# Attention and feed-forward kernel: dummy matmuls at the start, shared PSUM banks, q copies on ScalarE, fewer weight loads

## The chip, the cores and the metric

The kernel runs on one core of a Trainium2 chip. The metric is device time in microseconds (us), the median of several executions. The profile is of one execution; its span runs from the first to the last instruction and is shorter than the device time, by 1.7 to 3.8 us in the executions on record. "Clock" is the share of its full clock that TensorE was granted. Kernels are compared by a ratio: the mean time of one kernel's fast runs over that of the kernel before in the same rounds on the same chip, so it is not quite the ratio of the medians quoted beside it. 95% intervals are given in brackets.

## The reference

```python
# q, k, v: 4 batches x 8 heads x 768 positions x 64; heads 0, 2, 6 "retrieval", the others "streaming"
scores = q @ k.T / 8
mask   = causal                                        # retrieval heads
mask   = causal & (key < 4 | query - key < 64)         # streaming heads
a      = softmax(where(mask, scores, -1e9)) ; attn = a @ v
x      = attn, heads side by side: 3072 tokens x 512
h      = x @ w_in                                      # 512 -> 2048
out    = (max(h, 0) + alpha * min(h, 0)) @ w_out       # 2048 -> 512, fp32
```

## The kernel before

The work is cut into segments of one batch and two heads. Batch 0 is split into halves: segments 0 to 3 (kind "a") and 4 to 7 (kind "b"). Segments 8 to 19 are whole ("all"): 768 queries each. A segment passes through the engines like this: GpSimd casts q, k, v to bf16; TensorE transposes q and k; copies bring them from PSUM (the memory that TensorE writes to, in banks) to qT and kT; TensorE makes scores; ScalarE takes the exponential; VectorE multiplies the causal or window mask in; TensorE multiplies with v (`pav`); VectorE normalises (`xn`); TensorE transposes that, and VectorE copies it to xT. Blocks of the feed-forward are put between these pieces to fill TensorE.

The parts that the change and the argument touch:

```python
    def T_bank(nat, n, tag):                       # transposes of q or k
        tr = ps.tile([128, 1024], bf16, tag=tag, name="tr")
        for i in range(n):
            nc.tensor.transpose(tr[:, 128 * i:128 * (i + 1)], nat[:, i, :], ident)
        return tr

    def Tq(n):
        ...
        tr = T_bank(natq.pop(n), T, "mm0" if sg.kind == "a" else "tr")
        dst = qT[sg.seq % NK][:, sg.q0:sg.q1]
        if sg.kind == "all":
            nc.vector.tensor_copy(dst, tr[:, 0:S])
        else:
            nc.scalar.copy(...)

    def S_retr(n, hh, m):                          # scores of a retrieval head
        ...
        on_pe = sg.kind == "a"                     # mask added in PSUM by TensorE
        ...
        nc.scalar.activation(e[:, lo:hi], sc[:, 0:hi - lo], AF.Exp, scale=scale)
        for j in [] if on_pe else done:            # or multiplied by VectorE
            ej = e[:, sg.ro[j]:sg.ro[j] + RM[j]]
            nc.vector.tensor_tensor(ej, ej, mr[:, max(j - 1, 0), 0:RM[j]], op=ALU.mult)

    def AV(n, hh):
        pav = ps.tile([128, NT, D + 1], fp32, tag=f"pav{hh}", name="pav")
        ...
    def P2(t, s, quarter):                         # second product, and its output
        ...
            ot = work.tile([128, 512], fp32, tag="ot", name="ot", bufs=3)
            nc.scalar.copy(ot, po.pop(t))
            nc.sync.dma_start(out[r:r + 128, :], ot)
    ...                                            # main loop: casts for segment n + 2
            if i == 0:
                if 8 <= n + 2 < NSEG:
                    pre = [lambda n=n: cast(n + 2)]
```

The on_pe way matters later: TensorE adds a large negative number to the masked scores by one more matmul, so VectorE has no mask to multiply.

The softmax here doesn't subtract the row's maximum and nothing guards it: scores larger than these inputs give would overflow.

## Time and profile before

| | kernel before |
|---|---|
| device time, first three runs | 266.31 us (266.02 to 266.82) |
| span of the profiled execution | 263.8 us |
| TensorE busy | 238.1 us (90%) |
| VectorE, ScalarE, GpSimd busy | 181.3, 142.2, 68.1 us |
| TensorE idle in 5 to 22 us, 22 to 36, 36 to 60, 60 to 100 | 2.4, 2.3, 3.5, 5.9 us |

The lines behind these numbers are in the prediction. Read them in this order: the busy shares say that TensorE is the engine to free; the busy time by stretch says that its holes end at 100 us; its waits say who ends them.

### The profile page before, as it was taken

The numbers are of one execution on the slowest core, as the hardware profiler recorded it, in microseconds if no ns is written. First come the engines' busy times: TensorE is split into PE (matmuls) and PEld (weight loads), VectorE is DVE, ScalarE is ACT, GpSimd is POOL, SyncE is SP. The second block draws the span as 40 slices with busy tenths as digits, with TensorE's granted clock in tenths as the row PEclk, the third lists the DMA queues.
The fourth block names the chain that finished last, engine by engine and source line by source line (L and its number), as shares of the span: only waits on it lengthen the run. The fifth ranks groups of instructions, "written<-read, shape, count | busy, mean of one in ns | idle before, by whom it ended". The sixth has DMA issues, their size and how long they took to land.

```text
span 263.8 us, 5619 instructions
## 1 busy us (share of the span) xinstructions
PE 238.1 (90%) x2112; PEld 148.3 (56%) x2139; DVE 181.3 (69%) x483; ACT 142.2 (54%) x305; POOL 68.1 (26%) x122
## 2 busy tenths in 40 slices
PE   1897898978888879999999999999998999999994
PEld 1684345544766655655557855655557754456651
DVE  7897787557799776999528964997428946863310
ACT  2782675533675436686355646685446626644320
POOL 8799226524423422503113130500000000000000
PEclk9999999999999999999999999999999999999999
DMA  7989999999999978340121001000211011001212
GB/s 223 323 139 193 198 208 259 224 271 211 256 221 256 214 186 218 88 96 0 42 80 43 0 30 52 2 1 0 82 40 43 0 42 40 0 2 40 81 40 80
DMA packets 75275, 29.84 MB, mean 113 GB/s; under 512 B 63969, under 2 KB 72177, under 8 KB 75249
## 3 DMA queue, kind: packets, MB, share of 16 engines
q1 hardware_dynamic: 70448, 24.77, 37.2%
q0 software_dynamic: 4224, 4.19, 9.8%
q10 hardware_dynamic: 576, 0.53, 0.6%
q8 instruction: 16, 0.26, 0.5%
q14 instruction: 11, 0.08, 0.1%
HBM read 27.39 MB, written 6.29 MB: 128 GB/s over the span
## 4 chain that ended last, share of the span: by engine, by line
PE 63%; DVE 16%; DMA 7%; POOL 6%; ACT 4%; issue 3%; SPq 0%; POOLq 0%; ACTq 0%; DVEq 0%
PE mm L442 21%; PE mm L425 20%; PE sc L442 8%; DVE g L432 5%; PE pav L390 4%; DMA vf<-in_v_dram 4%; DMA kf<-in_k_dram 3%; PE sc L327 3%; PE tr L245 3%; DVE xn L397 2%; PE sc L359 2%; PE tr L405 2%; DVE eS L371 2%; ACT eR L334 2%; DVE eR L337 1%
## 5 line engine op out<-in xcount | busy, mean ns | idle before, releaser
L425 PE MATMUL mm<-xT,w_in_b 128*128 128x256 bf16 (+1 forms) x503 | 98.3, 325 | 3.8 <-DVE g L432 2.4
L432 DVE SCALAR_TENSOR_TENSOR g<-neg,oma,mm 128x512 bf16<-128x512 f32 (+1 forms) x128 | 77.3, 611 | 25.2 <-ACT neg L431 21.6
L431 ACT ACTIVATE neg<-mm 128x512 f32<-128x512 f32 (+1 forms) x128 | 62.6, 492 | 44.1 <-PE mm L425 40.8
L442 PE MATMUL mm<-w_out_b,g 128*128 128x512 bf16 x273 | 71.0, 379 | 0.8
L425 PEld LDWEIGHTS <-w_in_b 128*128 128x128 bf16 x512 | 47.6, 98 | 33.7 <-issue 5.0
L442 PEld LDWEIGHTS <-g 128*128 128x128 bf16 x384 | 34.8, 98 | 26.6
L334 ACT ACTIVATE eR<-sc 128x455 bf16<-128x455 f32 (+5 forms) x72 | 38.7, 552 | 18.8 <-PE sc L327 17.5
L366 ACT ACTIVATE eS<-sc 128x384 bf16<-128x384 f32 x60 | 28.8, 490 | 26.3 <-PE sc L359 24.1
L148 POOL CAST qb<-qf 128x768 bf16<-128x768 f32 (+1 forms) x16 | 12.5, 782 | 71.9 <-PE tr L245 65.0
L327 PE MATMUL sc<-qT,kT 128*128 128x268 bf16 (+16 forms) x141 | 25.8, 268 | 1.6 <-DVE kT L281 1.6
L337 DVE TENSOR_TENSOR eR<-eR,mr 128x128 bf16<-128x128 bf16 (+4 forms) x60 | 14.3, 257 | 16.6 <-ACT eR L334 16.5
L371 DVE TENSOR_TENSOR eS<-eS,ms 128x384 bf16<-128x384 bf16 x50 | 18.4, 375 | 8.5 <-ACT eS L366 8.1
L442 PE MATMUL sc<-w_out_b,g 128*128 128x512 bf16 x93 | 22.8, 379 | 0.1
L397 DVE TENSOR_TENSOR xn<-pav,rcp 128x448 bf16<-128x448 f32 (+2 forms) x40 | 21.8, 544 | 1.4
L359 PE MATMUL sc<-qT,kT 128*128 128x192 bf16 (+4 forms) x150 | 21.1, 234 | 0.4 <-ACT eS L366 0.4
L327 PEld LDWEIGHTS <-kT 128*128 128x128 bf16 x141 | 12.1, 99 | 11.8 <-DVE kT L281 2.0
L446 ACT COPY ot<-mm 128x512 f32<-128x512 f32 x18 | 10.6, 586 | 15.1 <-PE mm L442 14.7
L359 PEld LDWEIGHTS <-kT 128*128 128x128 bf16 x150 | 13.8, 99 | 6.0 <-issue 0.7
L149 POOL CAST kb<-kf 128x768 bf16<-128x768 f32 (+1 forms) x16 | 12.6, 786 | 11.2 <-PE tr L245 7.5
L390 PEld LDWEIGHTS <-eS 128*128 128x128 bf16 x270 | 11.6, 98 | 5.1 <-DVE eS L371 0.9
L407 DVE COPY xT<-tr 128x768 bf16<-128x768 bf16 (+2 forms) x20 | 9.5, 476 | 7.2 <-PE tr L405 7.0
L390 PE MATMUL pav<-vb,eS 128*128 128x65 bf16 x270 | 13.5, 194 | 0.7 <-DVE eS L371 0.4
(79 smaller groups left out, 199.3 us busy)
## 6 DMA issues: line engine op xcount, KB each, us to landing
out_dram<-ot SPq DMA_DIRECT2D x24, 256.0 KB
qf<-in_q_dram SPq DMA_DIRECT2D x12, 384.0 KB
kf<-in_k_dram SPq DMA_DIRECT2D x12, 384.0 KB
vf<-in_v_dram SPq DMA_DIRECT2D x24, 192.0 KB
w_in_b<-in_moe_w_in_dram POOLq DMA_DIRECT2D x4, 512.0 KB, 5.8
w_out_b<-in_moe_w_out_dram POOLq DMA_DIRECT2D x4, 512.0 KB, 13.1
qf<-in_q_dram SPq DMA_DIRECT2D x4, 256.0 KB
vf<-in_v_dram SPq DMA_DIRECT2D x5, 160.0 KB
```

The costliest lines, as they stand in the source:

```text
L327: nc.tensor.matmul(sc[:, a - lo:z - lo], kt[:, 128 * j:128 * (j + 1)], qt[:, c:c + z - a], start=True, stop=not masked)
L334: nc.scalar.activation(e[:, lo:hi], sc[:, 0:hi - lo], AF.Exp, scale=scale)
L337: nc.vector.tensor_tensor(ej, ej, mr[:, max(j - 1, 0), 0:RM[j]], op=ALU.mult)
L359: nc.tensor.matmul(sc[:, o:o + z - a], kt[:, 128 * j:128 * (j + 1)], qt[:, 124 * j + a:124 * j + z], start=True, stop=not on_pe)
L366: nc.scalar.activation(two, sc[:, 0:384].rearrange("p (s c) -> p s c", c=192), AF.Exp, scale=scale)
L371: nc.vector.tensor_tensor(two, two, ms5 if first == 4 else ms, op=ALU.mult)
L390: nc.tensor.matmul(pav[:, i, :], e[:, o:o + 128], vv[:, j, hh, :], start=(m == 0), stop=(m == len(terms) - 1))
L397: nc.vector.tensor_tensor(xn[n][:, lo:hi, 64 * hh:64 * hh + 64], pav[:, lo:hi, 0:D], rcp[:, lo:hi].to_broadcast([128, hi - lo, D]), op=ALU ...
L425: nc.tensor.matmul(psg[:, 0:w], w_in_b[:, a, 128 * f:128 * (f + 1)], xT[:, c, o:o + w], start=(c == 0), stop=(c == 3))
L431: nc.scalar.activation(neg[:, 0:w], psg[:, 0:w], AF.Relu, scale=-1.0)
L432: nc.vector.scalar_tensor_tensor(g_buf[t % 2][:, f, 0:w], neg[:, 0:w], oma[:, f:f + 1], psg[:, 0:w], op0=ALU.mult, op1=ALU.add)
L442: nc.tensor.matmul(po[t], g_buf[t % 2][:, f, 128 * s:128 * (s + 1)], w_out_b[:, f, :], start=(f == 0), stop=(f == 15))
```

## The change

Five things: 36 dummy matmuls during the first loads (so that the array's clock is up when the work begins), three PSUM banks in rotation for transposes and attention output together (instead of one bank for transposes and two for output), the q copies of whole segments on ScalarE, a reordered start of the first projection, and the weights in seven loads instead of eight, in another order.

```diff
-    def load_w_in(n):
+    def load_w_in(lo, hi):
...
+    def misc_tag():
+        n_misc[0] += 1
+        return f"m{n_misc[0] % 3}"
...
-        tr = ps.tile([128, 1024], bf16, tag=tag, name="tr")
+        tr = ps.tile([128, 1024], bf16, tag=tag or misc_tag(), name="tr")
...
-        tr = T_bank(natq.pop(n), T, "mm0" if sg.kind == "a" else "tr")
+        tr = T_bank(natq.pop(n), T, "mm0" if sg.kind == "a" else None)
...                                                 # Tk likewise
-            nc.vector.tensor_copy(dst, tr[:, 0:S])
+            nc.scalar.copy(dst, tr[:, 0:S])
...
-        pav = ps.tile([128, NT, D + 1], fp32, tag=f"pav{hh}", name="pav")
+        pav = ps.tile([128, NT, D + 1], fp32, tag=misc_tag(), name="pav")
...
+    warm = ps.tile([128, 512], fp32, tag="mm2", name="warm")
+    for i in range(36):
+        nc.tensor.matmul(warm[:, 0:128], ident, ident, start=True, stop=True)
     Tq(0)
...                                                 # w_in in three loads, then w_out, then the memsets
+    AV(3, 1)
+    for f in range(3):
+        P1(0, f, range(3))
+    X(3)
+    for f in range(3):
+        P1(0, f, range(3, 4))
+    for f in range(3, 6):
+        P1(0, f)
     nc.vector.tensor_copy(ms[:, 1, :], ms[:, 0, :])
...                                                 # three more mask copies
-    P1(0, 0, range(3))
-    P1(0, 1, range(3))
-    AV(3, 1)
-    P1(0, 2, range(3))
-    X(3)
-    ...
-    for f in range(3, 13):
+    for f in range(6, 13):
         P1(0, f)
```

More of the change, by code (lines that the diff above doesn't have):

```diff
@@ L231 @@
     oma = wpool.tile([128, 16], fp32, name="oma")
-    def load_w_in(n):
-        nc.gpsimd.dma_start(w_in_b[:, :, 512 * n:512 * (n + 1)],
-                            moe_w_in[:, 512 * n:512 * (n + 1)].rearrange("(a p) f -> p a f", p=128))
+    def load_w_in(lo, hi):
+        nc.gpsimd.dma_start(w_in_b[:, :, lo:hi], moe_w_in[:, lo:hi].rearrange("(a p) f -> p a f", p=128))
     def load_w_out(n):
@@ L239, in load_w_out @@
                             moe_w_out[512 * n:512 * (n + 1), :].rearrange("(a p) f -> p a f", p=128))
+    n_misc = [0]
+    def misc_tag():
+        n_misc[0] += 1
+        return f"m{n_misc[0] % 3}"
     def T_bank(nat, n, tag):
-        tr = ps.tile([128, 1024], bf16, tag=tag, name="tr")
+        tr = ps.tile([128, 1024], bf16, tag=tag or misc_tag(), name="tr")
         for i in range(n):
@@ L261, in Tk @@
         T = (sg.q1 - sg.q0) // 128
-        tr = T_bank(natk.pop(n), T, "mm1" if sg.kind == "a" else "tr")
+        tr = T_bank(natk.pop(n), T, "mm1" if sg.kind == "a" else None)
         for hh, h in enumerate(sg.heads):
@@ L402, in X @@
         nat = xn.pop(n)
-        tr = ps.tile([128, 1024], bf16, tag="tr", name="tr")
+        tr = ps.tile([128, 1024], bf16, tag=misc_tag(), name="tr")
         for i in sg.tiles:
@@ L483 @@
     cast_v(0)
+    load_w_in(0, 512)
     clear_e(nc.gpsimd, eS[1])
@@ L486 @@
     cast_v(1)
-    load_w_in(0)
+    load_w_in(512, 1024)
     cast_qk(3)
     cast_v(2)
-    load_w_in(1)
+    load_w_in(1024, 2048)
     clear_e(nc.gpsimd, eS[2])
     cast_v(3)
-    load_w_in(2)
-    load_w_in(3)
-    clear_k(nc.gpsimd, 4)
+    for i in range(4):
+        load_w_out(i)
     for i in range(NF):
         nc.gpsimd.memset(vf[i][:, 6, :, :], 0.0)
-    for i in range(4):
-        load_w_out(i)
+    clear_k(nc.gpsimd, 4)
     for n in range(4, 8):
@@ L516 @@
         if n == 0:
-            tra = ps.tile([128, 16], fp32, tag="tr", name="tra")
+            tra = ps.tile([128, 16], fp32, tag=misc_tag(), name="tra")
             nc.tensor.transpose(tra, alpha_r, ident_f)
             nc.vector.tensor_scalar(oma, tra, -1.0, 1.0, op0=ALU.mult, op1=ALU.add)
+    AV(3, 1)
[6 more added lines that the diff above has]
+        P1(0, f)
     nc.vector.tensor_copy(ms[:, 1, :], ms[:, 0, :])
@@ L526 @@
     nc.vector.memset(ms5[0:NSINK, 1, 148:152], 0.0)
-    P1(0, 0, range(3))
-    P1(0, 1, range(3))
-    AV(3, 1)
-    P1(0, 2, range(3))
-    X(3)
-    for f in range(3):
-        P1(0, f, range(3, 4))
-    for f in range(3, 13):
+    for f in range(6, 13):
         P1(0, f)
```

## The prediction

> **What bounds the kernel now.** I read the page's busy shares, then busy time by stretch, then TensorE's waits, then the timeline of TensorE, VectorE and ScalarE around each wait.
>
> ```profile
> PE 238.1 (90%) x2112; PEld 148.3 (56%) x2139; DVE 181.3 (69%) x483; ACT 142.2 (54%) x305; POOL 68.1 (26%) x122
> ```
>
> The span is 263.8 us (the device time of 266.31 adds a constant 2.5). TensorE is the bound: it executes one fixed order of matmuls, so the end moves by what its stalls and its slow clock lose, and by nothing else. Where are they?
>
> ```profile
> 5.00:22.00 17.00, 14.65 (x206) 12.26 (x208) 15.28 (x58) 12.55 (x29) 15.03 (x32) 1.00 1.06 231
> 22.00:36.00 14.00, 11.73 (x68) 5.39 (x67) 10.80 (x21) 7.12 (x14) 6.92 (x20) 1.00 1.21 205
> 36.00:60.00 24.00, 20.46 (x192) 12.03 (x194) 15.47 (x52) 12.86 (x29) 9.54 (x18) 1.00 1.14 243
> 60.00:100.00 40.00, 34.13 (x406) 24.92 (x411) 32.44 (x97) 21.53 (x53) 15.69 (x21) 1.00 0.96 225
> 100.00:199.00 99.00, 97.92 (x844) 59.27 (x856) 69.48 (x176) 58.10 (x119) 16.96 (x23) 1.00 0.17 49
> ```
>
> Columns: length, then busy time of PE, weight load, DVE, ACT, POOL. From 100 us on TensorE is full (97.92 of 99): nothing to win there. It has holes up to 100 us, and TensorE's own waits name them:
>
> ```profile
> PE tr L245 <- POOL qb L148: 5.4, 1, 5.4
> PE tr L245 <- DVE qT L254: 2.8, 4, 0.9
> PE tr L245 <- DVE xT L407: 2.6, 5, 0.9
> PE mm L425 <- DVE g L432: 2.4, 3, 1.1
> PE tr L405 <- DVE xn L397: 2.2, 4, 0.6
> ...
> PE tr L245 <- POOL vb L165: 0.8, 1, 0.8
> ```
>
> The first is the wait for the first load and cast. The next two are the single bank "tr": a transpose of q or k can't begin until the copy of the transpose before it has left the bank. The row "POOL vb" is one of these too: in the timeline the k transpose begins at 41.53, and the ScalarE copy that empties its bank ends at 41.12 + 0.37 = 41.49.
>
> ```profile
> 41.12 0.37 ACT L256 COPY qT<-tr 128x256 bf16<-128x256 bf16 x1
> ```
>
> The waits lose more than their idle time, since a transpose's modelled end overlaps the next start. Counting from issue to issue (start of the waiting instruction, less the start of the group before it and its count times the usual spacing), the stalls at "tr" are, in us: 1.00 (at 41.53), 0.67 (47.48), 1.01 (54.74), 0.63 (55.48), 0.66 (60.67), 0.85 (69.86), 1.14 (79.59), 0.84 (89.45), 0.81 (96.36), 0.81 (97.50), 0.36 (150.21). Sum 8.8.
>
> **The slow start.** Four transposes of q early, and the same four later; then VectorE while the early ones run:
>
> ```profile
> 8.81 0.63 PE L245 MATMUL tr<-ident,qb 128*128 128x128 bf16 x4
> 13.18 0.39 PE L245 MATMUL tr<-ident,qb 128*128 128x128 bf16 x4
> 7.23 0.62 DVE L281 COPY kT<-tr 64x512 bf16<-64x512 bf16 x1
> 10.73 0.65 DVE L506 MEMSET qT<- 128x144 uint32 x4
> 11.41 0.68 DVE L281 COPY kT<-tr 64x512 bf16<-64x512 bf16 x1
> ```
>
> The k transposes that follow begin at 9.24 and 13.40, so four take 0.43 early and 0.22 later: TensorE runs at half speed until about 11.7 us, although the granted-clock column says 1.00. But the second copy into kT begins at 11.41, though its transposes were over by 9.9: VectorE works through memsets without a hole from 5.4 on, and in the timeline it has none before 21.0.
>
> **What the Trainium skill says.** "TensorE: Matmul & The Clock Gate", Part 1, says that the array runs at half clock until some 3.4 us of sustained activity, and falls back after an idle window of about that length. The trace agrees: half speed, then full speed after roughly 4 us of unbroken work (7.9 to 11.7); the holes of about 1 us later don't bring it back. "ScalarE: Activation LUTs", What ACT_TABLE_LOAD costs, gives 186 ns + 0.833 ns per element for an ACTIVATE without pointer operands: 0.61 for 512 elements; the trace's qT copies took 0.59 (512) and 0.37 (256), so I extend those to about 0.81 for 768. "DMA: Bandwidth & Descriptors", Issuing engines are not separate DMA queues, says that all queues share 16 engines and interleave. The trace agrees in so far as the DMA share stays at 0.96 to 1.21 from 5 to 100 us with weights and q/k/v together. No page is needed for the bank wait: the trace has it.
>
> **The change, part by part.**
> Dummy matmuls: 36 of 128 columns at 0.108 each (0.43/4) are 3.9 us, begun when the identity is ready (1.4), over by 5.3; the first real transpose waits for a cast until 5.39 anyway. So they cost nothing, and TensorE then runs the next 6 us at twice the speed. What is it worth? In 7.9 to 11.7 about 1.9 us of TensorE time, but VectorE sets the pace of this stage: its order up to 22 us is unchanged in the built program, and it is full. TensorE gets early to the second segment's scores, which need the kT copy ending at 12.09 and began at 12.42. I give it 0.2 us.
>
> Order after the first batch: attention output of head pair 3 goes ahead of six partial projections, and four VectorE mask copies (22.84 to 24.22, that is 1.4 us) go behind the sixth g. Before, these copies held the reciprocal back to 24.22 and the output transposes to 24.99. Now nine partial projections (9 x 0.2155 = 1.9 us) come first; with the wait for the last exponential (22.5) I get transposes at 24.7: gain 0.3. But the copies now stand in the loop where a unit takes 0.862 on TensorE and g 0.75 on VectorE, with three banks in rotation, so hardly any slack (0.13). They take 0.8 to 1.4 there: loss 0.7. Net -0.4, a loss.
>
> Three shared banks: in the new rotation a bank comes back after three uses, so a transpose never waits for the one just before it, and the attention output gets banks whose readers are at least two steps back. All 8.8 us of stall lose their cause. What of it arrives? From 41 to 61 us VectorE is only two thirds busy, so of 3.97 I count 3.7. From 69 to 98 VectorE has no hole for 9 us at a time (67.7 to 77.1, 77.4 to 86.8): there TensorE, released earlier, meets VectorE at the next xn or mask, and the gain is what VectorE itself loses in work or idleness: 0.6, 0.75, 0.75 and 1.3 of 4.45, together 3.4. At 150: 0.2. Sum 7.3.
>
> q copies on ScalarE: 12 x 0.55 = 6.6 us off VectorE, 12 x 0.81 = 9.7 us onto ScalarE, which is 54% busy. It is what makes the 3.4 above possible (0.55 of each segment), so it is not counted again. After 100 us neither engine binds for long: 0.
>
> Weights in fewer parts: one issue less (0.74 on GpSimd), the first one 3 us earlier, w_out ahead of the memsets. GpSimd's work before the memset on which the later v loads wait changes by -0.74 - 1.65 + 2.98 = +0.6 us, and w_out is then ahead of those loads. But TensorE waits for no weight now, and the last casts of the second half end at 43.6 for transposes at 54.7. Value 0.
>
> Sum: 0.2 - 0.4 + 7.3 = 7.1 off. I keep about 15% back for waits that I don't see (ScalarE's longer copy ahead of an exponential, VectorE's order), so 6.1: 266.3 - 6.1 = **260.2 us**.
>
> **Rivals.** (a) VectorE becomes the bound of 60 to 100: it has 32.4 us of work in 40, less five q copies (2.8) 29.7; if its stretches without holes don't shrink, of 3.4 only half comes, and with the mask copies at their full 1.4 us the sum is 4: about 262.3. For it speaks the chain of waits, which has many VectorE pieces there; against it that TensorE's waits in it are for the two copies by name. (b) The warm clock counts in full: if VectorE's memsets are not what the first stage waits for, up to 1.9 us more: about 258.3. Against it stands the copy at 11.41. (c) Weights ahead of q/k/v make the second half's transposes wait at 36 to 55; each late load costs its lateness, 1 to 3 us: 261 to 263. Against it, 5 us and more of slack at each cast but the first.
>
> **Range and chances.** The stalls removed are certain as causes; what is open is how much is given back. 258.0 if the warm clock counts or nothing is given back, 263.0 if (a) and (c) both bite. 2% is 261.0, close above my figure: faster by over 2% 0.60, within 2% 0.39, slower 0.01.
>
> **What would show it right or wrong.** Right: TensorE's waits no longer name a q or k transpose waiting for qT or xT; early transposes 0.22 for four, yet the output of the first stage (TensorE's first projection, 22.0) moves by under 0.5; a stall of about 0.7 on "mm" behind g after the sixth unit; the stretch 36 to 100 shorter by about 7; a qT copy on ScalarE of about 0.81; the stretch from the last transposes to the end unchanged. Wrong: the first projection comes 1.5 us or more earlier (then VectorE wasn't the bound), TensorE's waits move to xn, kT or the exponentials with the same total, or casts wait for loads and transposes for casts.

## The result and the profile after

The changed kernel took 264.02 us (263.96 to 264.40, 4 runs) against 266.56 us for the kernel before in the same rounds: ratio 0.9908 [0.9885, 0.9931], that is 0.9% faster and within 2%. The span of the profiled execution was 262.4 us against 263.8: 1.4 us, where the medians differ by 2.5. (The profiled execution of the kernel before took 266.97 us, 3.2 more than its span; that of the changed kernel 264.40, 2.0 more. So about 1 us of the measured gain is not in these two profiles.) The prediction was 260.2 with a range from 258.0 to 263.0, so it is wrong by 3.8 us, and outside its range.

First, busy time by stretch of the changed kernel, with the columns of the prediction (length; PE, weight load, DVE, ACT, POOL; granted clock, DMA share, GB/s):

```profile
5.00:22.00 17.00, 14.58 (x212) 12.12 (x210) 15.29 (x58) 12.49 (x29) 15.03 (x33) 0.90 1.17 252
22.00:36.00 14.00, 12.01 (x69) 5.61 (x68) 9.94 (x21) 7.24 (x14) 6.17 (x17) 1.00 1.19 204
36.00:60.00 24.00, 22.82 (x225) 13.81 (x226) 16.81 (x57) 14.10 (x32) 11.50 (x21) 1.00 0.99 220
60.00:100.00 40.00, 32.60 (x380) 23.57 (x382) 32.79 (x92) 24.32 (x56) 13.66 (x19) 1.00 1.00 234
```

From 36 to 60 us TensorE is busy for 22.82 us where it was 20.46: that gain has come. From 60 to 100 us it is busy for 32.60, less than the 34.13 before, and VectorE, although 2.8 us of q copies have left it there, is no less busy (32.79 against 32.44).

TensorE's waits in the changed kernel (total, times, longest):

```profile
PE pav L395 <- DVE eS L376: 3.3, 5, 1.0
PE mm L430 <- DVE g L437: 2.6, 4, 1.1
PE sc L332 <- DVE kT L286: 1.9, 2, 1.6
PE tr L410 <- DVE xn L402: 1.6, 3, 0.5
PE warm L484 <- POOL ident masks.py:199: 1.4, 1, 1.4
PE pav L395 <- DVE eR L342: 1.3, 3, 0.5
PE sc L332 <- ACT eR L339: 1.1, 1, 1.1
```

No transpose of q or k waits for qT or xT any more. In their place stand waits for masked exponentials (eS, eR), that is, for VectorE and for what feeds it.

A third view makes the place of the loss plain: the start of the same matmuls in the timelines of several kernels, and by how many us each is earlier than in the kernel before. (X is the transpose of a segment's attention output, Tq the transpose of its q. The experiments are explained below.)

| start of | before, us | changed | six output buffers (e5) | casts moved too (e9) | masks on TensorE, q on VectorE (e15) | masks on TensorE in the kernel before (e17) | banks and masks alone (e18) |
|---|---|---|---|---|---|---|---|
| X of segment 3 | 24.99 | 0.37 | 0.37 | 0.35 | 0.38 | -0.05 | -0.05 |
| Tq of segment 4 | 36.44 | 0.13 | 0.13 | -0.02 | 0.13 | -0.04 | -0.04 |
| Tq of segment 8 | 60.67 | 3.61 | 3.78 | 3.40 | 3.61 | 0.27 | 3.37 |
| X of segment 8 | 66.26 | 3.61 | 3.77 | 3.16 | 3.55 | 0.22 | 3.31 |
| X of segment 9 | 75.92 | 1.15 | 2.54 | 2.31 | 3.91 | 0.34 | 3.67 |
| X of segment 10 | 85.66 | 0.31 | 1.48 | 1.98 | 4.28 | 0.86 | 4.04 |
| X of segment 11 | 95.16 | -0.21 | -0.17 | 1.97 | 4.77 | 1.35 | 4.52 |
| X of segment 12 | 102.88 | 0.97 | 1.01 | 3.15 | 5.94 | 1.34 | 5.70 |

In the changed kernel 3.6 us have been gained by 66 us, and 2.6 of them are lost by 103. From there to the end the two kernels run alike, but for another 0.4 us at the transposes near 150 us: the last X comes 1.38 us earlier, which is the difference of the spans. So the question is what took back the gain between 66 and 96 us.

The traces offered four suspects. **The output buffers**: an output copy on ScalarE stands for 1.48 us just there. It needs the buffer of the third output before it, whose transfer was issued late (at 60.93), behind loads that wait in the same queue. An exponential stands behind the copy. **The masks**: VectorE's masks became longer, at moments when GpSimd casts. **VectorE's queue as a whole**: from 67.5 to 75.2 us it has no hole. **The q copies**: on ScalarE one takes 0.80 us and stands ahead of the last exponential of a segment. A fifth one showed only in the experiments: **the clock** of the array.

Lines for the first two. ScalarE's output copy and TensorE's wait that follows from it, changed kernel, timeline (start, us, engine, line):

```profile
63.88 0.59 ACT L451 COPY ot<-mm 128x512 f32<-128x512 f32 x1 [1.48 <-PE sc L332]
64.97 0.35 PE L332 MATMUL sc<-qT,kT 128*128 128x106 bf16 x2 [1.14 <-ACT eR L339]
```

The bracket names a score matmul as the releaser of the copy, but with more buffers the wait is gone (run e5), so the name in the bracket is wrong. Now one pair of masks, first in the kernel before:

```profile
69.72 0.36 DVE L337 TENSOR_TENSOR eR<-eR,mr 128x140 bf16<-128x140 bf16 x2
```

Then in the changed kernel, with the casts beside it:

```profile
67.54 1.39 DVE L342 TENSOR_TENSOR eR<-eR,mr 128x140 bf16<-128x140 bf16 x2 [0.67 <-ACT eR L339]
67.14 0.83 POOL L149 CAST kb<-kf 128x768 bf16<-128x768 f32 x1
67.91 0.94 POOL L156 CAST vb<-vf 128x896 bf16<-128x896 f32 x1
```

The Trainium skill describes this: "SBUF — State Buffer", Who interferes with whom, says that a VectorE instruction with two SBUF inputs contends with a GpSimd instruction that reads SBUF, and in its next point, on the two-port modes, that whoever issues first holds the shared pair for the whole instruction while the other waits. The mask has two SBUF inputs, and this trace agrees with the contention: two masks took 0.36 us undisturbed and 1.39 while GpSimd cast. In the kernel before, VectorE was at g and at the copy of qT out of PSUM while the first cast ran (from 68.60, 0.90 us), and this pair of masks came in the pause before the next one (70.42). The casts begin when the transposes set their rows free: the new banks moved the transposes, and with them the casts, onto the masks.

### The profile page after: what moved, and what is told of

It is laid out like the page before. It is cut to its first block, busy times and chain, and to the rows that moved or that the text cites. A ratio compares the mean times of both kernels' runs of the same rounds, so it can differ in the third digit from the quotient of the medians.

```text
span 262.4 us, 5690 instructions
## 1 busy us (share of the span) xinstructions
PE 241.3 (92%) x2148; PEld 151.9 (58%) x2175; DVE 177.9 (68%) x471; ACT 150.1 (57%) x317; POOL 66.9 (25%) x121
## 3 DMA queue, kind: packets, MB, share of 16 engines
q1 hardware_dynamic: 70448, 24.77, 37.3%
## 4 chain that ended last, share of the span: by engine, by line
PE 68%; DVE 22%; ACT 5%; issue 3%; POOL 1%; ACTq 0%; POOLq 0%; DVEq 0%
PE mm L430 25%; PE mm L447 21%; PE sc L447 8%; DVE g L437 5%; PE pav L395 4%; PE sc L332 3%; DVE xn L402 3%; PE tr L410 3%; PE tr L250 2%; DVE eS L376 2%; PE sc L364 2%; ACT neg L436 2%; DVE eR L342 2%; ACT eR L339 2%; DVE kT L277 1%
## 5 line engine op out<-in xcount | busy, mean ns | idle before, releaser
L371 ACT ACTIVATE eS<-sc 128x384 bf16<-128x384 f32 x60 | 29.0, 493 | 19.9 <-PE sc L364 17.6
L342 DVE TENSOR_TENSOR eR<-eR,mr 128x128 bf16<-128x128 bf16 (+4 forms) x60 | 17.5, 310 | 19.9 <-ACT eR L339 19.8
L332 PE MATMUL sc<-qT,kT 128*128 128x268 bf16 (+16 forms) x141 | 25.4, 265 | 3.1 <-DVE kT L286 1.9
L332 PEld LDWEIGHTS <-kT 128*128 128x128 bf16 x141 | 12.0, 98 | 13.1 <-DVE kT L286 2.2
L395 PE MATMUL pav<-vb,eR 128*128 128x65 bf16 x336 | 13.6, 195 | 1.3 <-DVE eR L342 1.3
```

The costliest lines, as they stand in the source:

```text
L332: nc.tensor.matmul(sc[:, a - lo:z - lo], kt[:, 128 * j:128 * (j + 1)], qt[:, c:c + z - a], start=True, stop=not masked)
L371: nc.scalar.activation(two, sc[:, 0:384].rearrange("p (s c) -> p s c", c=192), AF.Exp, scale=scale)
L395: nc.tensor.matmul(pav[:, i, :], e[:, o:o + 128], vv[:, j, hh, :], start=(m == 0), stop=(m == len(terms) - 1))
```

## The experiments

Eighteen runs, all with correct outputs, in five rounds each. "Earlier" means the start of the same matmul in the profiled execution. The lines of code differ slightly from kernel to kernel, so L332 and L327 can be the same line.

**e1, the dummies alone** (kernel before, plus the 36 matmuls of the diff).

> The kernel before with the 36 dummy matmuls alone. Theory A (VectorE sets the pace of the first 22 us): ratio to before 1.000, within 0.2%, and the first projection still begins at 22.0 us. Theory B (the cold clock cost time): 1 to 2 us faster, ratio 0.993 to 0.996.

265.39 us against 265.81, ratio 0.9984 [0.9948, 1.0020]. Tq of segment 1 came 0.4 us earlier, X of segment 2 at 21.05 instead of 21.06, the first projection at 21.99. The dummies are worth nothing: theory A.

**e2, the shared banks alone** (kernel before, plus `misc_tag` in T_bank, AV, X and Tk/Tq).

> The kernel before with the three shared PSUM banks alone; the q copies stay on VectorE. Theory A (the bank stalls up to 60 us are really won, those from 60 to 100 us run into VectorE): the first full segment's q transposes (60.67 before) come at about 57.2, and 1.5 to 3 us of the 3.5 is still there at 100 us: 263.5 to 265. Theory B (ScalarE's q copies are what gives time back in the whole change): banks alone is faster than the whole change, 262.5 or less.

265.20 us, ratio 0.9973 [0.9929, 1.0017]. Tq of segment 8 came at 58.03, 2.6 us earlier than before; X of segment 12 at 102.87 against 102.88. All was given back between 64 and 97 us, in this execution with 1.7 us by a drop of the clock (see e5). Theory B is out; of theory A the direction came, but less was won at 60 us and less was left at 100 than it said.

**e3, the q copies on ScalarE alone.**

> The kernel before with the q copies of the full segments on ScalarE alone, one tr bank. Theory A (VectorE binds from 60 to 100 us, 0.55 us of it per segment goes): 1 to 2 us faster, 264.5 to 265.5. Theory B (the k transposes now wait for a 0.8 us copy queued behind exponentials on ScalarE): 0 to 1 us slower.

269.56 us, ratio 1.0137 [1.0097, 1.0177]: slower by 3.6 us, far more than even theory B allowed. In the trace X of segment 12 comes at 107.23, 4.35 us late, and 3.9 of these are lost after X of segment 8. A wait of the k transpose for the ScalarE copy is new, and the copy stands ahead of an exponential. TensorE's waits, then ScalarE's timeline:

```profile
PE tr L245 <- ACT qT L254: 1.1, 3, 0.5
```

```profile
92.33 0.81 ACT L254 COPY qT<-tr 128x768 bf16<-128x768 bf16 x1
93.05 0.55 ACT L334 ACTIVATE eR<-sc 128x455 bf16<-128x455 f32 x1
```

So the q copies alone, far from being what gives VectorE room, cost. (Of the 4.35 us, about 1.7 is a clock drop in the profiled execution from 87.5 to 91.0; see e5. In the three executions without one the span was 266.8 to 267.7, against a median of 264.0 for the kernel before, so the copies cost without it too.)

**e4, banks and q copies together**, neither dummies, order nor weights.

> Banks and q copies together, without the dummies, the new order and the new weight loads. If these three are worth nothing, the same as the whole change within 0.3%: 264.0 (ratio 0.991). If the weight loads ahead of q/k/v cost something from 60 to 100 us, it is faster than the whole change: 263 or less.

264.84 us, ratio 0.9946 [0.9914, 0.9978]. Beside the shared banks the q copies cost nothing any more. That they help there is not shown: the intervals of e2 and e4 overlap, and e2 had more clock drops (see e5). Together they are 0.4% away from the whole change and 4.6 us away from the prediction.

**e5, the whole change with six output buffers.**

```diff
-            ot = work.tile([128, 512], fp32, tag="ot", name="ot", bufs=3)
+            ot = work.tile([128, 512], fp32, tag="ot", name="ot", bufs=6)
```

> The whole change with six output buffers ot in place of three. Theory (the fourth output copy waits on ScalarE for the first output transfer, which stands in the sync queue behind loads, and holds back exponentials): the stall of 1.1 us on the scores at 64.97 goes, the q transposes of the second full segment come at about 64.4 in place of 65.60, and 0.5 to 1.2 us of it lasts: ratio to before 0.987. Rival (VectorE takes the same time anyway): transposes earlier, the end unchanged, ratio 0.991.

263.61 us, ratio 0.9894 [0.9861, 0.9928]: between theory and rival, and 0.4 us from the whole change, which the overlapping intervals do not tell from nothing. The wait is gone: the output copy now starts when its product is done.

```profile
62.49 0.58 ACT L451 COPY ot<-mm 128x512 f32<-128x512 f32 x1 [0.25 <-PE mm L447]
```

Tq of segments 9 and 10 came 1.4 us earlier than in the changed kernel. But Tq of segment 11 came at 86.98 against 87.02: the gain was gone within 12 us. The busy time of TensorE in four stretches of this run says how (length, busy time, granted clock, DMA share, GB/s):

```profile
76.20:79.60 3.40, 2.95 (x52) 1.00 1.18 285
79.60:83.05 3.45, 1.90 (x24) 1.00 1.15 259
83.10:86.50 3.40, 3.40 (x18) 0.50 1.00 227
86.60:90.00 3.40, 3.40 (x39) 1.00 0.98 221
```

After a stretch in which TensorE was busy for little more than half, its clock was halved for 3.4 us, and 18 matmuls filled the stretch where 39 fill the next. At half clock, 3.4 us lose 1.7. I looked for such drops in all profiles. Between 60 and 100 us there are more, each 3.4 us long at 0.50: 83.7 to 87.1 in e2, 87.5 to 91.0 in e3, 68.5, 85.5 and 99.2 in e6 (distances 17.07 and 13.66 us, five times and four times 3.41), 72.7 in e7, 94.9 in e11. None lies there in the profiled executions of the changed kernel or of the kernel before. In the first stage the changed kernel has one from 8.87 to 12.28, and so have seven other kernels with the dummies. So within an execution the drops start on a grid of 3.41 us, and its phase differs from execution to execution.

How often they come can be read from the mean clock of every execution. A drop of 3.41 us makes it about 0.993; 0.997 or more leaves no room for a whole one. Of 55 executions of the kernel before in the rounds of the experiments, 14 are at 0.994 or less, with spans of 265.2 to 265.8 us; the others have 263.5 to 265.1 (median 264.0). Of e2's six, five are at 0.994 or less (263.0 to 264.5), the sixth at 1.000 has 261.9. So the shared banks alone seem to be worth more than 0.7 us where no drop falls on them: 2.1 us of span, by that single execution. The drop of the first stage costs nothing: the changed kernel's four executions, with clocks from 0.990 to 1.000, have spans of 262.0 to 262.4. Of e5's six, three are at 1.000 (261.6 to 262.0), and only the slowest, the profiled one (0.987, 262.4), has the clock of two drops.

**e6 and e7, the casts for the next segments held back until the last causal mask** (e6 with three, e7 with six output buffers). GpSimd is made to read one element of that mask's result before it casts.

```diff
+    def touch(n):
+        nc.gpsimd.tensor_copy(tch, ebuf[n, 0][:, o:o + 1])
...
-            if i == 0:
+            if i == (len(seq_a(n)) if retr0 else 0):     # behind the last mask of segment n
                 if 8 <= n + 2 < NSEG:
-                    pre = [lambda n=n: cast(n + 2)]
+                    pre = [lambda n=n: touch(n)] if retr0 else []
+                    pre.append(lambda n=n: cast(n + 2))
...                                                 # then the load of a later segment, as before
```

> The whole change, with GpSimd's casts for the segment after next made to wait for the last causal mask on VectorE in segments whose first head is a retrieval head. Theory (the masks, with two SBUF inputs, are held up by casts that run at the same time): the excess of mask durations from 56 to 104 us, 4.8 us now, falls below 2, the kT copies come earlier, and the end by 2 to 3: ratio 0.982. Rival (VectorE is full there whatever the masks take; GpSimd's lateness moves the wait to the loads): excess falls, the end moves by under 0.5.

> Both repairs. If the two losses are separate, they add: 3 to 4 us below the whole change, ratio 0.977 to 0.980. If VectorE's work bounds this stretch, under 2 us.

e6: 271.33 us, ratio 1.0187 [1.0146, 1.0227]; e7: 267.34, ratio 1.0037 [1.0001, 1.0073]. Both missed, through a fault of the experiment: the casts came a whole segment later than before, loads and outputs behind them too (the wait of the exponential grew to 3.2 us in e6), and they met the masks of the streaming heads instead (a wait of 2.7 us for eS). The causal masks themselves were undisturbed: no longer than 0.23 us.

**e8, the whole change with the q copies back on VectorE.**

```diff
-            nc.scalar.copy(dst, tr[:, 0:S])
+            nc.vector.tensor_copy(dst, tr[:, 0:S])
```

> The whole change with the q copies of the full segments back on VectorE. From the runs of the parts (banks alone 0.9973, banks with q copies 0.9946): 0.7 us slower than the whole change. If the copy on ScalarE, ahead of the last exponential, costs as much as VectorE wins: the same.

263.79 us, ratio 0.9902 [0.9867, 0.9937], not to be told from the whole change. In it the q copies on ScalarE are worth nothing.

**e9, six output buffers and the casts moved with care**: for segment n + 3, right behind the k transposes' pieces of segment n + 1 and the last causal mask of segment n. **e10**: as e9, with the cast of v apart, behind `xn` of the segment before.

```diff
-            if i == 0:
-                if 8 <= n + 2 < NSEG:
-                    pre = [lambda n=n: cast(n + 2)]
...                                                 # cast(n + 2) stays for n = 6, 7, 8
+            if n >= 8 and n + 3 < NSEG and i == after_tk(n):
+                pre = [lambda n=n: touch(n)] if RETR[SEGS[n].heads[0]] else []
+                pre.append(lambda n=n: cast(n + 3))            # e10: cast_qk(n + 3)
+            # e10 only: at i == 2, touch_xn(n) and cast_v(n + 3)
```

> The whole change with six output buffers (so that no exponential waits for an output transfer), and with GpSimd's casts for a segment moved: they start right after the last causal mask of the segment three before it, where VectorE does some 2.4 us of copies out of PSUM, instead of when the transposes set the rows free, which is just when the masks run. Theory (the masks are held up while GpSimd reads SBUF, and that took back what the shared banks gave between 60 and 100 us): the excess of the masks' durations over their undisturbed ones between 56 and 104 us falls from 5.4 us (run with six buffers alone) to under 2, the X transposes of segment 12, at 101.87 us there, come 1 to 3 us earlier, and the time is 261 to 262.5. Rival (the masks are not what PE waits for in the end; the exponentials and the weight of VectorE's other work set the pace, and the array's clock takes the rest): excess falls, X of segment 12 within 0.7 us of 101.9, time 263 to 264.

> As the run before it, but the cast of v (0.8 us, a third of the three) apart from those of q and k, at the start of a segment behind the normalised rows, so that GpSimd has 1.6 us of reading after the last mask rather than 2.4 and does not reach into the masks of the streaming head. Theory: excess of the masks under 1.2 us, X of segment 12 another 0 to 1 us earlier than with the three casts together, time 260.5 to 262. Rival: same as the run before it within 0.4 us.

e9: 262.91 us, ratio 0.9874 [0.9848, 0.9900]; e10: 262.75, ratio 0.9862 [0.9836, 0.9888]. The causal masks (VectorE's instructions on eR between 57 and 97 us: count, then min/median/max ns), changed kernel and then e9:

```profile
L342 DVE TENSOR_TENSOR eR<-eR,mr x18: 215/228/961, 61.7 to 89.8; 128x128 bf16<-128x128 bf16 x6, 128x132 bf16<-128x132 bf16 x3, 128x136 bf16<-128x136 bf16 x3, 128x140 bf16<-128x140 bf16 x3
```

```profile
L342 DVE TENSOR_TENSOR eR<-eR,mr x18: 212/228/232, 62.1 to 87.7; 128x128 bf16<-128x128 bf16 x6, 128x132 bf16<-128x132 bf16 x3, 128x136 bf16<-128x136 bf16 x3, 128x140 bf16<-128x140 bf16 x3
```

The longest fell from 961 to 232 ns; part of the disturbance moved to the streaming masks: over both kinds, from 56 to 104 us, the time above the undisturbed one fell from 5.4 us (e5) to 2.6, not under 2. X of segment 12 came 2.1 us earlier than in e5, but about 1.7 of that is e5's clock drop. The ratios say 0.5 us (0.9894 to 0.9874), and their intervals overlap. e10 is within 0.4 us of e9, as its rival had it. So the collisions are real, and what they cost alone is small, if anything: closer to the rival than to the theory.

**e11, four clearings of qT (0.65 us) moved from VectorE's first stage to GpSimd.**

```diff
+    for i in range(1, NK):                        # behind clear_k(nc.gpsimd, 4)
+        nc.gpsimd.memset(qT[i][:, SPLIT:S + 32], 0.0)
-    for i in range(1, NK):
-        nc.vector.memset(qT[i][:, SPLIT:S + 32], 0.0)
```

> The whole change, with four clearings of qT (0.65 us of VectorE together) moved from VectorE's first stage to GpSimd, behind all that is urgent there. If VectorE's copies bound the first 21 us, as the prediction said to explain that dummies are worth nothing, the X transposes of segment 2 (21.05 us in the changed kernel) come 0.4 to 0.7 us earlier, and the time is 263.4 to 263.8 against 264.0. If something else does (landing of the loads, the exponentials), they come at 21.0 and the time is 264.0.

276.43 us, ratio 1.0371 [1.0330, 1.0411]. The edit was at fault: the scores of the first stage read these columns, and GpSimd cleared them only at 25 us.

```profile
PE sc L364 <- POOL qT L509: 10.8, 1, 10.8
```

Up to that wait it answers its question all the same: X of segment 0 came at 13.88 instead of 14.50, which is the 0.65 us taken from VectorE. VectorE does pace the first stage up to there.

**e12, e5 with 14 dummy matmuls in each of three holes near 70, 80 and 90 us.**

```diff
+            if i == 2 and n in (8, 9, 10) and not RETR[sg.heads[hh]] and RETR[sg.heads[0]]:
+                for _ in range(14):
+                    nc.tensor.matmul(bank[:, 392:512], ident, ident[:, 0:120], start=True, stop=True)
...                                                 # pav is now a part of the tile bank
```

> The whole change with six output buffers, and 14 dummy matmuls of 120 columns (0.75 us of the array) in each of the three places around 70, 80 and 90 us where PE stands for about 1 us before the second tile of a streaming head. What is tested: in the run with six buffers the granted clock was 0.50 from 83.05 to 86.55 us, one stretch of 3.4 us, 1.7 us of array time, after a stretch of 3.4 us in which PE was busy for 1.86. Such stretches begin on a grid of 3.41 us whose phase differs from run to run, so a hole that costs nothing in one execution costs 1.7 us in another. Theory (clock drops after thinly used stretches between 68 and 92 us cost part of the gain, on the average of executions): no drop between 60 and 100 us in the profiled execution, spread of the executions under 0.7 us instead of 1.3, median 262.3 to 263.0 against 263.6. Rival (the dummies stand in the way and the drops are rare): median 263.6 to 264.3, spread as before.

263.24 us, ratio 0.9880 [0.9857, 0.9903]. No drop between 60 and 100 us, and the spread of six executions was 0.44 us (262.96 to 263.40) where e5 had 1.34 (262.95 to 264.29). The slow executions are gone, the fastest is where it was; the median lies between theory and rival. But the clock accounts for e5's slowest execution alone: its three at clock 1.000 have 261.6 to 262.0 us, e12's three have 261.0 to 261.4. And the ratios (0.9894 and 0.9880) are not told apart. So what the drops cost e5 on the average is not shown; by its one execution in six it would be about 0.3 us (an estimate: 1.7/6).

**e13, e5 with the causal masks of segments 8 to 11 on TensorE**; **e14**, the same with e12's dummies; **e15**, e13 with the q copies on VectorE.

```diff
-        on_pe = sg.kind == "a"
+        on_pe = sg.kind == "a" or n in (8, 9, 10, 11)
```

> The whole change with six output buffers, and the causal masks of the retrieval heads of segments 8 to 11 added by TensorE in the score bank instead of multiplied by VectorE: VectorE is freed of some 5 to 8 us between 60 and 95 us (0.25 to 0.4 us for each of about 18 masks undisturbed, and 4.4 us of excess), TensorE gets about 18 matmuls of 128 to 144 columns, 1.1 us. Theory (VectorE sets the pace from 60 to 100 us, so what the shared banks free there goes into its queue): the X transposes of segment 12 come at 97 to 99 us (101.87 with six buffers alone, 1.7 of it a clock drop), and the time is 260 to 261.8. Rival (exponentials, or the order of work on TensorE, set the pace, and VectorE only looks it): X of segment 12 at 99.6 to 101, as with the moved casts, time 262.5 to 263.5.

> As e13, with the 14 dummies in each of three waits. If clock drops between 60 and 95 us still occur in some executions of e13, the spread here is smaller (under 0.6 us) and the median 0 to 0.5 us lower; if the holes are gone with the masks, the dummies only stand in the way: 0 to 0.6 us slower.

> As e13, with the q copies of the full segments on VectorE again (0.55 us each there, 0.80 on ScalarE). With the masks on VectorE they were worth nothing. If VectorE is what sets the pace, they cost now what they add on VectorE less what they free ahead of the exponentials: within 0.5 us of e13, and I lean to faster by 0.2, as ScalarE's exponentials are on the chain once the masks are gone.

e13: 260.33 us, ratio 0.9771 [0.9735, 0.9807]. e14: 260.57, ratio 0.9788 [0.9749, 0.9827]. e15: 259.29 (259.16 to 259.37), ratio 0.9735 [0.9700, 0.9769]. Eighteen masks, some 4 us of VectorE undisturbed, moved to TensorE for about 1 us there (an estimate: 18 matmuls, 0.06 us apart in the timeline of the first stage), and the time fell by 3.3 us against e5. X of segment 12 came at 97.41. This is the theory's number, not the rival's. The dummies are of no use here (e14 is 0.2 us slower). And with room on VectorE the q copies are better on it by 1.0 us, more than expected; in the same rounds no execution of e15 is as slow as any of e13. That on ScalarE they hold up exponentials is read from the traces, not tested apart. The stretch from 60 to 100 us in e15, and the first three of TensorE's waits of the whole run:

```profile
60.00:100.00 40.00, 37.13 (x440) 26.93 (x438) 31.15 (x86) 24.98 (x58) 13.77 (x19) 1.00 1.08 254
```

```profile
PE mm L430 <- DVE g L437: 2.4, 3, 1.1
PE sc L332 <- DVE kT L286: 1.9, 2, 1.6
PE pav L395 <- DVE eS L376: 1.8, 4, 0.5
```

TensorE is busy for 37.13 of 40 us, 4.5 more than in the changed kernel, and no wait for eR is left. In the chain of waits between 62 and 100 us, added up by engine, VectorE has 20.8 us, TensorE 8.0 and ScalarE 7.8 in the changed kernel; in e15 15.6, 17.6 and 4.2. In the kernel before it was 19.6, 12.1 and 5.1: VectorE held most of this chain before the change as well.

**e16, the reordered start alone.** (The diff of the change from `AV(3, 1)` on.)

> The kernel before with the reordered start of the projection alone (three blocks and the rest ahead of the mask copies). In the whole change it brought the first q transposes of segment 4 from 36.44 to 36.31 us, where the prediction had -0.4 (a loss). Theory: alone it does the same, 36.3 +- 0.1, and 0.0 to 0.2 us of time; the four mask copies take about 0.6 us. Rival (the prediction's own reckoning): 36.8 and 0.4 us slower.

265.77 us, ratio 0.9991 [0.9951, 1.0032]. Tq of segment 4 came at 36.66, 0.22 us later than before, X of segment 3 at 24.77, 0.22 earlier: for the start of segment 4 nearer to the rival, for the time (the same) nearer to the theory.

**e17, e13's masks in the kernel before; e18, shared banks, six output buffers and these masks, and nothing else of the change.** (Edits as above.)

> The kernel before, with the causal masks of the retrieval heads of segments 8 to 11 added by TensorE. Theory (VectorE's room and the shared banks need each other: with the old banks each transpose still waits for the copy of the one before it, at the same q copies on VectorE): the stretch between the X transposes of segments 8 and 12 shrinks from 36.6 us to 34 to 35.5, and the time is 263.5 to 265; the shared banks, with what comes with them, are then worth 4 to 5.5 us beside it (259.3). Rival (the masks alone are the gain, the banks give what e2 showed, under 1 us): 260 to 261.5.

> Shared banks, six output buffers and the masks on TensorE, without the dummies, the reordered start, the q copies on ScalarE and the merged weight loads. Expected if those four are worth nothing beside it: within 0.5 us of 259.3. If the merged weight loads or the reorder carry a part of the gain up to 57 us (the first q transposes of a full segment came at 57.06 us in the whole change, at 58.03 with the banks alone): 259.8 to 260.6, with the 1 us already there at 57 us.

e17: 264.45 us, ratio 0.9935 [0.9903, 0.9967]. e18: 259.64, ratio 0.9761 [0.9726, 0.9796]. By the ratios, of 266 us, the masks alone bring 1.7 us, the shared banks alone 0.7 (e2, not told from nothing), both with the buffers 6.4. By the spans of executions without a clock drop it is 1.3, 2.1 (a single execution) and 6.4: still three us more together than apart. Both runs came as their theories said. Six buffers with the old banks were not run. But in e17's trace no output copy waits for a buffer (before 110 us it starts at most 0.44 us after ScalarE's last instruction, each time released by its own product), while the transposes still wait at the single bank (2.3 us for xT, 1.3 and 1.2 for qT), and in e18 they don't. Busy time from 60 to 100 us, e17 and then e18:

```profile
60.00:100.00 40.00, 36.11 (x437) 26.52 (x435) 30.35 (x83) 22.33 (x54) 15.97 (x21) 1.00 0.99 231
```

```profile
60.00:100.00 40.00, 37.13 (x445) 27.01 (x443) 31.16 (x86) 24.74 (x58) 14.03 (x19) 1.00 1.04 242
```

e15, which has the dummies, the reorder and the weight loads beside what e18 has, is 0.4 us from it by the medians and 0.7 by the ratios, whose intervals overlap: that these parts together are worth anything is not shown.

## Why the prediction was wrong

Right in mechanism and size:

- **The stalls at the bank** are gone from TensorE's waits, all of them. Between 41 and 61 us the prediction counted 3.7 us; the table shows 3.61 - 0.13 = 3.5.
- **The dummies**: 0.2 predicted, 0.0 measured (e1). The early transposes ran at full speed and nothing came of it, since VectorE's copy started at the same time as before (lines below). Not foreseen in the changed kernel: the array fell back to half clock at 8.87, between the two groups of four, and stayed there until 12.28. e1 is the clean test: there the clock stayed full (four k transposes at 8.89 in 0.38 us), and what TensorE gained became a wait for VectorE's kT (the last line below; before, the same matmul began at 12.42). Rival (b), that the warm clock counts in full, is false.
- **The weights**: 0 predicted, and no wait for them appeared. What e15 and e18 leave for them and the two parts above is 0.4 us by the medians, 0.7 by the ratios, and not clear of noise. Rival (c) did not happen.
- **A q copy on ScalarE**: 0.81 us predicted, 0.80 measured.

The dummies, transposes on either side of the fall of the clock, and VectorE's copy, from the changed kernel's timelines; then the score matmul of e1:

```profile
1.43 4.02 PE L484 MATMUL warm<-ident 128*128 128x128 bf16 x36 [1.43 <-POOL ident masks.py:199]
8.40 0.39 PE L250 MATMUL tr<-ident,qb 128*128 128x128 bf16 x4
8.90 0.59 PE L250 MATMUL tr<-ident,kb 128*128 128x128 bf16 x4
11.40 0.68 DVE L286 COPY kT<-tr 64x512 bf16<-64x512 bf16 x1
```

```profile
12.14 0.35 PE L327 MATMUL sc<-qT,kT 128*128 128x430 bf16 x1 [0.75 <-DVE kT L281]
```

Wrong in size: **the reorder**. Predicted -0.4 (gain 0.3, loss 0.7). In the whole change the gain at X of segment 3 was 0.37 and 0.13 of it was left at 36 us; alone 0.22 became -0.22 (e16). The four mask copies took 0.5 us in the changed kernel (31.50 to 32.02), not 0.8 to 1.4; what stretched them at the old place was not tested. Timeline of VectorE, kernel before and then changed kernel, the first two of the four each:

```profile
22.84 0.59 DVE L521 COPY ms<-ms 128x192 bf16<-128x192 bf16 x1
```

```profile
31.50 0.20 DVE L537 COPY ms<-ms 128x192 bf16<-128x192 bf16 x1
```

**The step that failed** is the one that runs "From 69 to 98 VectorE has no hole for 9 us at a time" to "together 3.4". Where it expected 3.4 us of gain, the changed kernel lost 2.6 (3.61 to 0.97 in the table). That is a swing of 6.0 us. In all, the profiles' gain of 1.4 falls 5.7 short of the predicted sum of 7.1, so the other terms nearly balance. Its reading that VectorE has no hole from 67.7 to 77.1 holds but for one of 0.22 us at 68.4. The step saw that TensorE, released earlier, would meet VectorE, and then credited the path with what VectorE was to lose in work. It failed in three ways:

1. VectorE lost no work. The q copies went (2.8 us in this stretch), and longer masks came: added over the masks from 56 to 104 us, their time above the undisturbed one was 1.5 us before and 4.8 after (5.0 in e2 and 4.0 in e3, so either part alone brings it). The casts begin when transposes free their rows, so an earlier transpose is an earlier cast; this second-order effect is missing from the step. By itself it is worth some 0.5 us, not clear of noise (e9 against e5); the masks' own time stays there.
2. Work taken from VectorE was put on ScalarE, which stood earlier in the same chain. "It is what makes the 3.4 above possible" is refuted: e8 is as fast as the whole change, e3 is slower than the kernel before, and e15 beats e13.
3. The chain between 60 and 100 us belongs to VectorE in the changed kernel, and what TensorE no longer lost at the banks became idleness before VectorE's results. Relieving VectorE of the masks shows it: 3.3 us came at once (e13), twice as much as the same relief gave beside the old banks (1.7, e17). Banks and buffers are worth 4.8 us beside it (264.45 to 259.64), where the banks alone were worth 0.7, or 2.1 without clock drops. The prediction had named this among the signs of being wrong: TensorE's waits moved to the exponentials, as VectorE masks them.

Two smaller things may have taken their part. The wait for the output buffer cost 1.4 us in the trace and some 0.4 in the ratios, not clear of noise (e5). Drops of the clock after thinly filled stretches took nothing from the profiled execution of the changed kernel, where none lies after 12.28 us until the very end; they do cost the kernel before 1.4 us in a quarter of its executions, and e5 about as much in one of six. The prediction's remark that holes of about 1 us do not bring the half clock back is wrong in some executions. The 15% kept back for "ScalarE's longer copy ahead of an exponential, VectorE's order" named the right waits, and held back 1.0 us where 3.8 more were missing.

**Rival (a)**, that VectorE becomes the bound from 60 to 100 us, was the true one. It was too mild: it left half of the 3.4, hence 262.3, and did not reckon with a loss.

What stays open. How the loss from 66 to 96 us divides among masks, q copies and clock can't be read off as a sum: the effects feed one another. Even with VectorE relieved, the shared banks gain little in the stretch itself: from Tq of segment 8 to X of segment 12 e17 takes 41.1 us and e18 39.9, so 1.3 us, not 3.4. What else bounds it there, with TensorE busy for 37.13 of 40, I have not taken apart. The share of weights, reorder and dummies in what e15 and e18 leave isn't known either; the merged loads were not run alone.

A version that beats both kernels came out of it: e15, 259.29 us, 2.65% faster than the kernel before and 1.7% faster than the changed one (0.9735 / 0.9908).

## What to carry to other kernels

When a wait is removed in a stretch where a second engine has no holes, count as gain only what that engine can deliver earlier, and ask what the earlier release sets off: here it moved casts onto masks and copies ahead of exponentials. Before moving work off a full engine, follow the chain to see whether the other engine stands earlier in it; a mask that TensorE can add in PSUM freed VectorE where a copy moved to ScalarE did not. And judge a change of 1% by several executions, because one profile can hold a clock drop of 1.7 us that the next one lacks.

## What the Trainium skill lacked or had wrong

- "TensorE: Matmul & The Clock Gate", Part 1, lets the array fall back to half clock after an idle window of about 3.4 us, and calls the window free-running. The grid agrees (drops begin at multiples of 3.41 us apart: 17.07 and 13.66 in e6). But no window was idle: in five windows followed by a drop TensorE was busy for 1.74 to 1.88 of 3.41 us in the records (one each of e2, e3, e5, e6, e7), and two windows of much the same kind, 1.87 (e5, at 25 us) and 1.69 (e7, at 93 us), were not followed by one. Part 1 does say of one kernel that short pauses between groups of matmuls made the clock go back and forth, but the page gives no share below which a window counts as idle, and the records here don't settle it.
- No page says how often equal executions of one kernel differ by such a drop: here 14 of 55 executions of the kernel before have a clock of 0.994 or less, and are 1.4 us longer (medians of the spans, 265.4 and 264.0).
- "SBUF — State Buffer", Who interferes with whom, agrees, but the section's only sizes are two ratios, for a VectorE and a GpSimd measurement that it doesn't describe: here a causal mask of 128x140 went from about 0.23 to as much as 0.96 us beside casts of 0.82 to 0.94 us.
- No page says that a mask can be added in PSUM by an identity matmul to relieve VectorE; in e13 eighteen masks moved so brought 3.3 us against e5.
